# Issuing a weight piece's store, and the load that follows it, one place later in a pair

## The chip, the cores and the metric

One core of one Trainium2 chip. The metric is device time in microseconds (us) of one execution; a kernel is compared by the median of its runs. The engines are named as in the profile: PE (TensorE, its weight loads PEld), DVE (VectorE), ACT (ScalarE), POOL (GpSimd) and SP (SyncE, which here does nothing but issue transfers; its rows carry the name SPq).

## The reference, cut to what matters

A retention layer makes 2304 rows of 512 columns; a first mixture of four experts runs every row through every expert; a second mixture routes each row to one of eight experts by a greedy assignment.

```
x   = retention(q, k, v)                      # (2304, 512)
out = sum_e p[:, e] * (relu(x @ w1[e]) @ w2[e])          # first MoE, E = 4, F = 1024
logits = out @ w_gate ; assigned = greedy(logits)        # 2304 / 8 rows for each expert
out2[mask_e] = relu(out[mask_e] @ w1b[e]) @ w2b[e]       # second MoE, E = 8
```

All of it is float32.

## The kernel before

**The split.** PE works here on a reduced format, so a float32 operand is held as two tiles: a high half (ACT copies it, which rounds) and a low half (POOL or DVE subtracts). A product is then three matmuls: high by high, low by high, high by low.

**The stage of the change** is the first MoE. Its rows go through in three passes `u` of 768 rows. In a pass, 16 "pairs" `kk` follow each other; `k = 16 u + kk` counts them through (0 to 47). A pair is a quarter of an expert's hidden columns: seven block products P, Q, R of a two-by-two block scheme, in steps `a` to `g` (line L677, 6 matmuls each), and three second-layer tiles `py` (L727, 12 matmuls each) of pairs that came before, which stand after steps b, d and e. ACT copies the running sums out of the accumulators (`sum`, L684: after steps a, c and e) and makes the hidden halves (`h`, L694). Step f adds to the accumulator P that the third of these copies reads, so PE starts step f only after it. For the next pairs the kernel also prepares weights: `w1_load` (L376, L379: tiles `r`, `tw`), their split (L398, L399: `wah`, `wth`, `wbh` on ACT, `wal`, `wbl` on POOL, `wtl` on DVE), and the second-layer weights, two loads `w2_load(k, 0)` and `w2_load(k, 1)` (L659, tile `r`; `r2` in the program) and two splits `w2_split` (L664 ACT, L665 POOL or DVE).

**The job that the change touches.** While PE works on the first MoE, the weights of the second MoE are split ahead, in 128 pieces `c` of 128 x 512 (64 in pass 0, 64 in pass 1). For each piece: a load `pv` (256 KB, L433), the high half on ACT (L447) and the low half on POOL (L448), both into a tile `pair`, and a store: both halves (512 KB, L453, shown as `w_halves`) for a first-layer piece, the low half alone (256 KB, L455, `w_low`) for a second-layer piece. Eight pieces of the one kind are followed by eight of the other. The generator `halves` does, at one call: split piece `c`; store piece `c - 1`; load piece `c + 2`. It is called by `spare(True)` at five places of a pair, called A (after step a), C (ahead of step c), D (after step d), E (after step e) and E' (ahead of step f) here. `spare(False)` stands at four further places: behind `w2_load(k, 0)`, after step c, after step d, after step f; in this stage it does nothing. Tiles `pv` and `pair` have three buffers each, so the load of piece `c + 2` takes the place of piece `c - 1`.

**What sets the order.** The program is written out in the order of the loop body; each engine works through its own list in that order and waits at an instruction until what it needs is there. All transfers named here are issued by SP in one list, and all go through one queue (q1). Other members of that list are `w1_store` in pass 0 (L383, L384, `w_sums`: it follows place D and stores tiles that DVE makes), the block sums of the next pass (L869 stores, L872 to L888 loads, called behind steps c and f), and the result rows `x_rows` (L745), which wait for DVE's last addition to a row tile.

Of the kernel before, what the change touches and what calls it, by code (L numbers as in the profile page):

```python
# [327 lines left out]
def tile_kernel(ctx, tc, a, x1d, xs, ss, ts, w1s, w2s, out):  # L328
# [17 lines left out]
    if True:  # L346
# [79 lines left out]
        def piece_of(c):  # L426
            e, i = divmod(c // 2, 8)
            return e, i, slice(c % 2 * HW, c % 2 * HW + HW)

        def halves_load(c):  # L430
            e, i, o = piece_of(c)
            r = room[0].tile([128, HW], F32, name="pv")
            nc.sync.dma_start(r, (a["w1b"] if i < 4 else a["w2b"])[e, i % 4][:, o])  # L433
            HV[c] = r

        def halves(c0, c1, loaded=False):

            if not loaded:
                for c in range(c0, min(c0 + HA, c1)):
                    halves_load(c)  # L440
                yield
                yield
            for c in range(c0, c1 + 1):
                if c < c1:
                    r = HV[c]
                    pair = HV[c] = room[0].tile([128, 2, HW], F32R, name="pair")
                    nc.scalar.activation(pair[:, 0], r, AF.Copy)  # L447
                    nc.gpsimd.tensor_tensor(pair[:, 1], r, r32(pair[:, 0]), op=OP.subtract)  # L448
                if c > c0:
                    e, i, o = piece_of(c - 1)  # L450
                    pair = HV.pop(c - 1)
                    if i < 4:
                        nc.sync.dma_start(w1s[e, i][:, :, o], r32(pair))  # L453
                    else:
                        nc.sync.dma_start(w2s[e, i - 4][:, o], r32(pair[:, 1]))  # L455
                if c + HA < c1:
                    halves_load(c + HA)
                yield
# [179 lines left out]
        with ExitStack() as st:  # L638
# [17 lines left out]
            def w2_load(q, i):  # L656
                e, j = divmod(q % 16, 4)
                W2[q, i] = [hp.tile([128, 512], F32, name="r2", bufs=2)]
                nc.sync.dma_start(W2[q, i][0], a["w2a"][e, 2 * j + i])  # L659
# [190 lines left out]
            later = late()  # L850
            HC = 64
            jobs = [halves(0, HC, True), halves(HC, NH)]

            def spare(main):

                if not open_ or k < 2:
                    return
                if k > 16 * NP1 - 16:
                    next(later, None)
                elif main:  # L860
                    next(jobs[min(u, 1)], None)


            BLOCKS = {0: (0, 0), 1: (0, 1), 2: (1, 1)}
# [33 lines left out]
            for k in range(NPAIR):  # L898
                u, kk = divmod(k, 16)
# [12 lines left out]
                def block(i):  # L912
                    raw[i] = room[0].tile([128, 2, TG], F32, name=f"raw{i}")
                    if i in BLOCKS:
                        row, col = BLOCKS[i]
                        nc.sync.dma_start(raw[i], xs[u, :, 2 * col:2 * col + 2, row * TG:(row + 1) * TG])
                    else:
                        nc.sync.dma_start(raw[i], ss[u, i - 3])
# [7 lines left out]
                if k not in (1, NPAIR - 1):  # L926
                    step(k, "a")
                if turn_:
                    for _ in jobs[u]:
                        assert False  # L930
                    for _ in sums_of[u]:
                        assert False
                    st_p.close()
                    open_ = False
                    room[0] = pool(st_p, f"blocks{u}")
                    w2_load(k, 0)
                    for i in (0, 1, 4):
                        block(i)
                full = lone
                if k:  # L940
                    put(k - 1, 0, 1, "R")
                spare(True)
                step(k, "b")
                if not turn_:
                    w2_load(k, 0)
                spare(False)
                put(k, 0, 0, "Q")
                if not open_ and kk == 0:
# [4 lines left out]
                if turn_:  # L953
                    for i in (3, 5, 2, 6):
                        block(i)
                spare(True)
                step(k, "c")
                some(10 if full else 3)
# [76 lines left out]
    with ExitStack() as st:  # L1035
# [388 lines left out]
        for n, t in enumerate(range(NT - LATE, NT)):  # L1424
# [10 lines left out]
            else:  # L1435
                x = last[t - NT + K1]
# [80 lines left out]
```

## Time and profile before

| | us |
|---|---|
| median of 3 runs | 1157.22 (1154.66 to 1160.98) |
| the profiled execution | 1154.98 |
| its span | 1153.2 |
| PE busy | 1133.4 (98%) |
| ACT, POOL, DVE busy | 561.2, 632.0, 705.6 |
| q1, share of 16 engines' span | 69.3% |

The profiled execution is 1.8 us longer than its span and 2.2 us under the median. PE is busy nearly always by the page, but pipelined matmuls hide short stops in such a sum; the distance from one pair to the next shows them.

### The profile page before, as it was taken

The numbers are of one execution on the slowest core, as the hardware profiler recorded it, in microseconds if no ns is written. First come the engines' busy times: TensorE is split into PE (matmuls) and PEld (weight loads), VectorE is DVE, ScalarE is ACT, GpSimd is POOL, SyncE is SP. The second block draws the span as 40 slices with busy tenths as digits, with TensorE's granted clock in tenths as the row PEclk, the third lists the DMA queues.
The fourth block names the chain that finished last, engine by engine and source line by source line (L and its number), as shares of the span: only waits on it lengthen the run. The fifth ranks groups of instructions, "written<-read, shape, count | busy, mean of one in ns | idle before, by whom it ended". The sixth has DMA issues, their size and how long they took to land.

```text
span 1153.2 us, 22293 instructions
## 1 busy us (share of the span) xinstructions
PE 1133.4 (98%) x8007; PEld 988.5 (86%) x8007; DVE 705.6 (61%) x1632; ACT 561.2 (49%) x1262; POOL 632.0 (55%) x563
## 2 busy tenths in 40 slices
PE   9999999999999999999999999999999999999997
PEld 7878899989898998988899999998987888788886
DVE  4696777767665444544456777776347766666421
ACT  3444555555565555555554666666430333333341
POOL 4551576677774576666645999998231112222311
PEclk9999999999999999999999999999999999999999
DMA  9675699999994889898974655555214877788690
GB/s 330 219 248 176 234 338 344 322 319 321 345 309 144 279 286 335 290 310 302 316 262 158 221 181 195 192 180 158 78 55 167 311 292 284 307 332 334 252 409 27
DMA packets 131056, 292.99 MB, mean 254 GB/s; under 512 B 14849, under 2 KB 26881, under 8 KB 126849
## 3 DMA queue, kind: packets, MB, share of 16 engines
q1 hardware_dynamic: 127584, 281.88, 69.3%
q0 software_dynamic: 3216, 9.67, 2.4%
q8 instruction: 63, 1.03, 0.4%
q14 instruction: 49, 0.39, 0.1%
q10 hardware_dynamic: 144, 0.02, 0.0%
HBM read 214.41 MB, written 77.33 MB: 253 GB/s over the span
## 4 chain that ended last, share of the span: by engine, by line
PE 56%; DMA 15%; issue 5%; POOL 5%; DVE 3%; ACT 3%; SPq 3%; POOLq 0%; ACTq 0%; DVEq 0%
PE py L727 16%; PE ph L227 10%; PE P L677 9%; PE py L227 8%; PE R L677 5%; DMA r<-in_w2a 4%; DMA pv<-in_w1b 3%; DMA pv<-in_w2b 3%; DMA tw<-w_sums 3%; PE Q L677 2%; POOL pair L448 2%; PE pr L227 2%; DMA r<-in_w1a 1%; POOL w2l L665 1%; ACT pair L447 1%
## 5 line engine op out<-in xcount | busy, mean ns | idle before, releaser
L727 PE MATMUL py<-w2h,h 128*128 128x512 f32 x1056 | 349.5, 391 | 0.9 <-ACT h L694 0.8
L727 PEld LDWEIGHTS py<-w2h,h 128*128 128x128 f32 x1056 | 198.2, 188 | 40.4 <-ACT h L694 1.7
L448 POOL TENSOR_TENSOR pair<-pv,pair 128x512 fp32r<-128x512 f32 x128 | 177.3, 1391 | 97.4 <-ACT pair L447 93.4
L727 PE MATMUL py<-w2l,h 128*128 128x512 f32 x528 | 206.3, 391 | 0.0
L399 POOL TENSOR_TENSOR wal<-r,wah 128x512 fp32r<-128x512 f32 x48 | 66.8, 1392 | 87.1 <-ACT wah L398 71.8
L727 PEld LDWEIGHTS py<-w2l,h 128*128 128x128 f32 x528 | 99.2, 188 | 16.0
L684 ACT ACTIVATE sum<-P 128x384 f32<-128x384 f32 x144 | 70.0, 486 | 87.1 <-PE P L677 86.7
L665 POOL TENSOR_TENSOR w2l<-r,w2h 128x512 fp32r<-128x512 f32 x64 | 85.7, 1338 | 44.7 <-ACT w2h L664 44.7
L447 ACT ACTIVATE pair<-pv 128x512 fp32r<-128x512 f32 x128 | 80.2, 627 | 55.6 <-DMA pv<-in_w1b 27.2
L734 DVE SCALAR_TENSOR_TENSOR acc<-py,pr,acc 128x512 f32<-128x512 f32 x115 | 85.6, 745 | 29.8 <-PE py L727 29.5
L399 DVE TENSOR_TENSOR wtl<-tw,wth 128x768 fp32r<-128x768 f32 x48 | 63.5, 1322 | 64.4 <-ACT wth L398 64.2
L827 POOL TENSOR_TENSOR pp<-pw,wgb 128x512 f32<-128x512 f32 x64 | 98.5, 1560 | 1.4 <-DMA r<-in_w2a 1.4
L399 POOL TENSOR_TENSOR wbl<-r,wbh 128x512 fp32r<-128x512 f32 x48 | 81.1, 1690 | 14.6 <-ACT wbh L398 11.2
L695 DVE SCALAR_TENSOR_TENSOR h<-Q,h 128x384 fp32r<-128x384 f32 x96 | 53.4, 556 | 51.2 <-ACT h L694 51.2
L227 PE MATMUL ph<-gh,ub 128*128 128x288 f32 x512 | 83.3, 300 | 0.4 <-DVE gl L254 0.4
L664 ACT ACTIVATE w2h<-r 128x512 fp32r<-128x512 f32 x96 | 60.2, 628 | 42.2 <-DMA r<-in_w2a 42.1
L227 PEld LDWEIGHTS ph<-gh,ub 128*128 128x128 f32 x512 | 72.2, 188 | 1.2 <-DVE gl L254 0.7
L1299 POOL DMA_INDIRECT xg<-x_rows,idx x14 | 15.9, 1135 | 100.5 <-DVE idx L254 65.6
L534 ACT ACTIVATE Y<-s 64x128 f32<-64x128 f32 x128 | 33.8, 270 | 59.0 <-PE s L525 55.1
L694 ACT ACTIVATE h<-Q 128x384 fp32r<-128x384 f32 x96 | 46.7, 486 | 30.5 <-DVE Q L688 29.7
L507 POOL TENSOR_TENSOR Y<-Y,gk 64x576 f32<-64x576 f32 (+2 forms) x36 | 38.6, 1091 | 36.7 <-DMA Y<-in_kv 28.2
L523 PE MATMUL s<-X,Y 64*64 64x64 f32 x576 | 56.7, 228 | 2.0 <-DVE X L536 1.2
(272 smaller groups left out, 2667.7 us busy)
## 6 DMA issues: line engine op xcount, KB each, us to landing
w_halves<-pair SPq DMA_DIRECT2D x64, 512.0 KB, 6.0
ub<-w_halves SPq DMA_DIRECT2D x32, 1024.0 KB, 9.5
r<-in_w2a SPq DMA_DIRECT2D x96, 256.0 KB, 5.1
r<-in_w1a SPq DMA_DIRECT2D x64, 256.0 KB, 4.9
pv<-in_w1b SPq DMA_DIRECT2D x64, 256.0 KB, 5.6
pv<-in_w2b SPq DMA_DIRECT2D x64, 256.0 KB, 5.4
w_low<-pair SPq DMA_DIRECT2D x64, 256.0 KB, 4.8
raw<-in_w2b SPq DMA_DIRECT2D x32, 512.0 KB, 7.5
```

Source lines behind the costliest of these rows:

```text
L227: self.add("pe", cost, lambda: self.nc.tensor.matmul(out, w, x, start=start, stop=stop, **kw), (w, x), (out,), chain=chain, cols=self.size(x))
L399: low = lambda e, i, x: lambda: e.tensor_tensor(w(i, 1), x(), r32(w(i, 0)), op=OP.subtract)
L447: nc.scalar.activation(pair[:, 0], r, AF.Copy)
L448: nc.gpsimd.tensor_tensor(pair[:, 1], r, r32(pair[:, 0]), op=OP.subtract)
L523: nc.tensor.matmul(score()[:, h], Y[lo, h, ch(c + 1)], X[lo, h, ch(c + 1)], start=True, stop=True)
L664: nc.scalar.activation(h, r, AF.Copy)
L665: (nc.vector if i and q < 2 * NPAIR // NP1 else nc.gpsimd).tensor_tensor(lo, r, r32(h), op=OP.subtract)
L677: nc.tensor.matmul(PS[k][o][:, :TG], wx[:, c:c + 128], xx[:, kk], start=(start and n == 0), stop=(stop and n == 5), skip_group_check=True)
L684: nc.scalar.activation(sums[n], PS[k]["P"][:, :TG], AF.Copy)
L727: mm(y, x, w, start=(start and n == 0), stop=(stop and n == len(todo) - 1), **kw)
L734: nc.vector.scalar_tensor_tensor(x, y, s, x, op0=OP.mult, op1=OP.add)
L827: nc.gpsimd.tensor_tensor(pp, w[g, f], G0[e], op=OP.mult)
```

## The change

The generator yields once more, between the split of a piece and its store and load. `spare` notes that a store and a load are owed, and issues them at the next place at which it is called, whichever it is. Every piece still has the same instructions; PE, DVE, ACT and POOL have the same lists as before. Only SP's list is in another order.

```
@@ -446,6 +446,7 @@
                     pair = HV[c] = room[0].tile([128, 2, HW], F32R, name="pair")
                     nc.scalar.activation(pair[:, 0], r, AF.Copy)
                     nc.gpsimd.tensor_tensor(pair[:, 1], r, r32(pair[:, 0]), op=OP.subtract)
+                yield True
                 if c > c0:
                     e, i, o = piece_of(c - 1)
                     pair = HV.pop(c - 1)
@@ -851,14 +852,22 @@
             HC = 64
             jobs = [halves(0, HC, True), halves(HC, NH)]
 
+            owed = []
+
             def spare(main):
 
                 if not open_ or k < 2:
                     return
                 if k > 16 * NP1 - 16:
                     next(later, None)
-                elif main:
-                    next(jobs[min(u, 1)], None)
+                elif main or owed:
+
+                    job = jobs[min(u, 1)]
+                    if owed:
+                        owed.pop()
+                        next(job, None)
+                    if main and next(job, None):
+                        owed.append(True)
 
 
             BLOCKS = {0: (0, 0), 1: (0, 1), 2: (1, 1)}
@@ -926,8 +935,8 @@
                 if k not in (1, NPAIR - 1):
                     step(k, "a")
                 if turn_:
-                    for _ in jobs[u]:
-                        assert False
+                    owed.clear()
+                    assert not [x for x in jobs[u] if x]
                     for _ in sums_of[u]:
                         assert False
                     st_p.close()
```

**SP, beginning of pair 24 (pass 1).** Before; `r2` are the two second-layer weight loads, the first store and load are those issued at place A, the last two those of place C:

```order
L379 DMA tw_5668<-w1_sums 128x768
L453 DMA w1_halves<-pair_5641 256x1x512
L433 DMA pv_5687<-in_w1b 128x512
L659 DMA r2_5696<-in_w2a 128x512
L659 DMA r2_5714<-in_w2a 128x512
L453 DMA w1_halves<-pair_5683 256x1x512
L433 DMA pv_5720<-in_w1b 128x512
```

The same place of the changed program:

```order
L379 DMA tw_5668<-w1_sums 128x768
L660 DMA r2_5693<-in_w2a 128x512
L454 DMA w1_halves<-pair_5641 256x1x512
L433 DMA pv_5696<-in_w1b 128x512
L660 DMA r2_5714<-in_w2a 128x512
L454 DMA w1_halves<-pair_5683 256x1x512
L433 DMA pv_5736<-in_w1b 128x512
```

The first `r2` has moved ahead of A's store and load.

**SP, middle of pair 10 (pass 0).** Before; the stores and loads are those of places C, D and E, with a store of the block sums and `w1_store` (two rows) between them:

```order
L455 DMA w2_low<-pair_3305 128x512
L433 DMA pv_3342<-in_w2b 128x512
L869 DMA x_sums<-cx_2938 128x384
L455 DMA w2_low<-pair_3338 128x512
L433 DMA pv_3380<-in_w2b 128x512
L383 DMA w1_sums<-r1_3290 128x512
L384 DMA w1_sums<-tw_3358 128x768
L455 DMA w2_low<-pair_3376 128x512
```

The same place of the changed program:

```order
L878 DMA x_sums<-cx_2935 128x384
L456 DMA w2_low<-pair_3305 128x512
L433 DMA pv_3361<-in_w2b 128x512
L383 DMA w1_sums<-r1_3290 128x512
L384 DMA w1_sums<-tw_3355 128x768
L456 DMA w2_low<-pair_3338 128x512
L433 DMA pv_3396<-in_w2b 128x512
L456 DMA w2_low<-pair_3376 128x512
```

D's store and load have moved behind `w1_store`, C's behind the block sum.

**SP, pair 17, the first of pass 1 with pieces.** Before; `x1_rows` are result rows, the three stores and loads those of D, E and E':

```order
L453 DMA w1_halves<-pair_4522 256x1x512
L433 DMA pv_4560<-in_w1b 128x512
L745 DMA x1_rows<-acc4_1744 128x512
L453 DMA w1_halves<-pair_4556 256x1x512
L433 DMA pv_4602<-in_w1b 128x512
L745 DMA x1_rows<-acc5_1745 128x512
L453 DMA w1_halves<-pair_4598 256x1x512
```

The same place of the changed program:

```order
L746 DMA x1_rows<-acc4_1744 128x512
L454 DMA w1_halves<-pair_4522 256x1x512
L433 DMA pv_4588<-in_w1b 128x512
L746 DMA x1_rows<-acc5_1745 128x512
L454 DMA w1_halves<-pair_4556 256x1x512
L433 DMA pv_4636<-in_w1b 128x512
L454 DMA w1_halves<-pair_4598 256x1x512
```

Each result row has moved ahead of one store and load.

## Rows read from the trace of the kernel before

**Rows 1.** The page: span, and PE's busy time, share and instructions.

```profile
span 1153.2 us, 22293 instructions
PE 1133.4 (98%) x8007; PEld 988.5 (86%) x8007; DVE 705.6 (61%) x1632; ACT 561.2 (49%) x1262; POOL 632.0 (55%) x563
```

**Rows 2.** Timeline of PE, step b of pairs 2, 3, 15, 20, 30: start, length, what.

```profile
126.29 0.51 PE L677 MATMUL Q<-x1h,wah 128*128 128x384 f32 x2
...
141.77 0.51 PE L677 MATMUL Q<-x1h,wah 128*128 128x384 f32 x2
...
330.32 0.51 PE L677 MATMUL Q<-x1h,wah 128*128 128x384 f32 x2
...
416.77 0.51 PE L677 MATMUL Q<-x1h,wah 128*128 128x384 f32 x2
...
576.91 0.51 PE L677 MATMUL Q<-x1h,wah 128*128 128x384 f32 x2
```

**Rows 3.** Waits of PE's weight loads, 126 to 331 us: total, times, longest.

```profile
PEld P L677 <- ACT sum L684: 2.1, 3, 1.3
PEld R L677 <- DVE Q L688: 1.1, 2, 0.9
```

**Rows 4.** The same, 416 to 577 us.

```profile
PEld P L677 <- ACT sum L684: 5.8, 7, 1.3
```

**Rows 5.** Timeline of all engines in pair 24: in brackets idle time and its ender.

```profile
482.68 0.54 SPq L453 DMA_DIRECT2D w_halves<-pair  x1
...
483.93 2.04 SPq L659 DMA_DIRECT2D r<-in_w2a  x2
...
487.97 0.85 ACT L398 ACTIVATE wth<-tw 128x768 fp32r<-128x768 f32 x1 [1.01 <-DMA tw<-w_sums]
...
488.73 0.61 ACT L398 ACTIVATE wbh<-r 128x512 fp32r<-128x512 f32 x1
...
489.42 1.55 POOL L399 TENSOR_TENSOR wbl<-r,wbh 128x512 fp32r<-128x512 f32 x1 [1.08 <-ACT wbh L398]
...
490.52 0.63 ACT L664 ACTIVATE w2h<-r 128x512 fp32r<-128x512 f32 x1 [1.18 <-DMA r<-in_w2a]
...
491.06 0.61 ACT L447 ACTIVATE pair<-pv 128x512 fp32r<-128x512 f32 x1
...
491.23 1.27 POOL L665 TENSOR_TENSOR w2l<-r,w2h 128x512 fp32r<-128x512 f32 x1 [0.27 <-ACT w2h L664]
...
491.58 0.47 ACT L684 ACTIVATE sum<-P 128x384 f32<-128x384 f32 x1
...
492.10 0.62 PE L677 MATMUL P<-x2h,wth 128*128 128x384 f32 x2 [0.41 <-ACT sum L684]
...
493.79 0.54 SPq L453 DMA_DIRECT2D w_halves<-pair  x1
```

**Rows 6.** Timeline in pairs 10 and 11: SP, ACT, POOL, PE.

```profile
261.00 0.33 SPq L433 DMA_DIRECT2D pv<-in_w2b  x1
...
263.00 0.32 SPq L384 DMA_DIRECT2D w_sums<-tw  x1
...
266.32 0.63 ACT L447 ACTIVATE pair<-pv 128x512 fp32r<-128x512 f32 x1
...
269.13 2.59 POOL L448 TENSOR_TENSOR pair<-pv,pair 128x512 fp32r<-128x512 f32 x2
...
270.81 0.51 PE L677 MATMUL P<-x4h,wth 128*128 128x384 f32 x2
```

**Rows 7.** Line L433 (the loads `pv`), all 128: time from issue to landing.

```profile
DMA to landing us min/median/max: 2.9/5.4/7.4
```

**Rows 8.** Timeline of SP in pair 17.

```profile
377.35 0.54 SPq L453 DMA_DIRECT2D w_halves<-pair  x1
...
381.45 0.33 SPq L745 DMA_DIRECT2D x_rows<-acc  x1
```

**Rows 9.** Stretches: length, busy time by engine, PE's clock share, DMA share, GB/s.

```profile
141.77:157.25 15.48, 15.48 (x80) 14.04 (x79) 11.29 (x18) 9.06 (x17) 11.06 (x9) 1.00 1.00 365
```

More of the change, by code (lines that the diff above doesn't have):

```diff
@@ L448, in halves @@
                     nc.gpsimd.tensor_tensor(pair[:, 1], r, r32(pair[:, 0]), op=OP.subtract)
+                yield True
                 if c > c0:
@@ L852, in tile_kernel @@
             jobs = [halves(0, HC, True), halves(HC, NH)]
+            owed = []
             def spare(main):
@@ L859, in spare @@
                     next(later, None)
-                elif main:
-                    next(jobs[min(u, 1)], None)
+                elif main or owed:
+                    job = jobs[min(u, 1)]
+                    if owed:
+                        owed.pop()
+                        next(job, None)
+                    if main and next(job, None):
+                        owed.append(True)
             BLOCKS = {0: (0, 0), 1: (0, 1), 2: (1, 1)}
@@ L928, in tile_kernel @@
                 if turn_:
-                    for _ in jobs[u]:
-                        assert False
+                    owed.clear()
+                    assert not [x for x in jobs[u] if x]
                     for _ in sums_of[u]:
```

## The prediction

> **What bounds the kernel now.** The page first: PE is busy 98% of 1153.2 us [rows 1], so only work taken from PE, or stops of PE, can move the time; the change takes no work away. The stops have to be looked for in the stage where SP's list changes, and busy time hides them there. The second view is therefore the timeline of PE at one fixed instruction of each pair, the first matmul of step b. An undisturbed pair takes 141.77 - 126.29 = 15.48 us [rows 2]. In pass 0, pairs 2 to 14 take 330.32 - 126.29 = 204.03 us, 13 x 15.48 would be 201.24: 2.8 us are lost. In pass 1, pairs 20 to 29 take 160.14 us instead of 154.8: 5.3 us are lost. Together 8.1 us, 0.7% of the kernel, and that is all that a better order of transfers can return. The third view, PE's waits, says for what it stops: for ACT's copy `sum` of accumulator P, seven times in pass 1 [rows 4], three times in pass 0, where step g also waits twice for DVE [rows 3].
>
> The fourth view shows why the copy is late: all engines in pair 24 [rows 5]. ACT stands idle 1.18 us until a second-layer weight of the first MoE (`r`, the first of SP's two loads at 483.93) has landed. Only then come `w2h` at 490.52, place D's `pair` at 491.06 and `sum` at 491.58, and PE's step f goes on at 492.10. That load was issued behind place A's store (482.68) and A's load `pv`. The stop thus ends with a transfer, and the change moves exactly this one two places forward in SP's list.
>
> **What the move ahead of A's store is worth.** `tw`, which stands just before A's store, lands when `wth` starts (487.97), the weight when `w2h` starts (490.52) [rows 5]: 2.55 us for store, load and weight, 512 + 256 + 256 KB. If they land in the order of issue, the weight, with a quarter of these bytes, lands after 0.64 us, near 488.6. ACT reaches it when `wbh` is done, near 489.3, so the wait of 1.18 us is gone. But the next thing on ACT is place D's `pair`, and its `pv` is the load of place A. It now lands last of the three, where the weight landed before: 490.5. So the stall is passed on: not the weight is late next, but D's piece. What is won is the slot that `w2h` took behind the landing, 491.06 - 490.52 = 0.54 us: `pair` at 490.5, `sum` at 491.0, PE at 491.6 instead of 492.1.
>
> There is a second, smaller gain. SP's next burst of transfers starts with place E's store (493.79), which waits for POOL's low half of D's piece. POOL goes `wbl` (ends 490.97), `w2l` after 0.27 us of waiting for ACT's `w2h`, `pair`, then the store [rows 5]. With `w2h` early POOL runs on from `wbl`: the burst starts 0.27 us sooner, and in pass 1, where a late burst makes the next `tw` and weight late, this adds up.
>
> *Pass 1.* The lag that makes the seven stops is carried from pair to pair, so the 0.54 us counts once and the 0.27 us up to seven times: 0.54 + 7 x 0.27 = 2.4 us. Against it stands the start of pass 1. E's store stood ahead of a result row and left at 377.35; now it stands behind one that SP issues at 381.45, when DVE's addition is done [rows 8]. Its store and load, 768 KB, have to go in the burst that follows. At the 365 GB/s of the fullest pair [rows 9] these are 2.15 us at most; nothing, if the queue was empty anyway. I take 1.0, about the middle, since the trace has no row for it. Pass 1 gives 1.4 us; its bounds are nothing (2.4 less 2.15, and less than that if the 0.27 is not passed on) and all 5.3.
>
> *Pass 0.* Here the stops stand alone. The three waits for `sum` sum to 2.1 us with 1.3 as the longest [rows 3], so the other two together are 0.8. Cut by 0.54 each, they return 0.54 from the longest and at most 0.8 from the others: 1.3; the waits of step g for DVE, 1.1 us in two, come from the same late `sum` and shrink with it. PE loses 2.8 in all; I take half, 1.4. Bounds: 0.5 (one slot) and 2.8.
>
> **What the moves behind other transfers cost.** In pass 0, D's store and load now stand behind `w1_store`, whose second row SP issues at 263.00 when DVE has made the tile. D's load left at 261.00 before [rows 6]; with `w1_store` and the store of about 0.33 us each ahead of it, it leaves near 263.8, 2.8 us later. Its user is the copy of place E' (266.32, no wait: the load took under 5.3 us). Behind that copy on ACT stand the hidden half `h` of step f and the first `sum` of the next pair, and PE's step c of that pair needs this `sum` at 270.81. Copy, `h` and `sum` take about 0.63 + 2 x 0.49 = 1.6 us, so the load may land until 269.2, 5.4 us after its issue. On POOL the piece has its turn only at 269.13, 2.8 us after the copy began, behind `wbl`; that cover hides all but a few tenths. I cost this move at nothing: the same bytes stand ahead of the load as before, minus 2.8 us in which the queue went on, so it should land sooner after its issue than the 5.3 us it had. If it doesn't, PE pays in each of twelve pairs (the last loads nothing); this is the rival below.
>
> The Trainium skill, "DMA: Bandwidth & Descriptors", section "Rules for kernel authors", advises to issue a transfer early and to wait for it late. The change does the opposite for every `pv`, and the rule counts against it. By that rule the time is the slower rival's below. No row so far shows ACT stopping PE at place E', so the rule and these rows differ.
>
> C's pair of transfers moves behind a stored block sum, whose tile DVE has made one place before, and E' behind up to three loads of 192 KB in a few pairs. At 365 GB/s the three take 1.6 us [rows 9]. What they make late is the next pair's place C, whose copy is followed by `sum` for step e; step e is two steps and a `py` later. Costed at nothing. SP's own time is no matter: the same rows are issued.
>
> **The sum.** 1.4 + 1.4 = 2.8 us. Against the profiled execution's own time that is 1154.98 - 2.8 = 1152.2, against the median of runs, 2.2 us higher, 1154.4. The three runs lie 6.3 us apart, so neither is better; I forecast the middle, **1153.3 us**.
>
> **Rivals.**
> - *All stops go.* If the weight's landing is the only link and D's `pv` is not missed (landing nearly together with the weight), and the bursts move forward by more than 0.27, then all 8.1 us return: 1146.9 from the profiled time, 1149.1 from the median. For it: ACT's wait before `w2h` is in each stopped pair the last one. Against it: D's copy follows the weight at once, and its load now lands last.
> - *The order doesn't matter because the transfers are the bound.* Pair 3 moves 365 GB/s with the DMA engines busy throughout [rows 9]. If the stopped pairs lack bandwidth and not order, the gain is the slot alone, 0.5 us and less: 1154.5 from the profiled time, about 1156.5 from the median. Against it: pair 3 takes 15.48 us all the same [rows 2]. The Trainium skill, same page, section "Specifications", gives about 358 GB/s as a core's share of memory bandwidth; the row lies at that.
> - *Slower: D's load lands too late for the next pair.* Its place is E' of pass 0, its point of decision a landing 5.4 us after issue. The median of all `pv` is just that, the longest 7.4 [rows 7]. At 6.4, midway, PE stops 1.0 us in each of twelve pairs: 12 us more, less the 2.8: about 1164. At 7.4 it would be 24 us. For it: the rows of all places leave no margin. Against it: the load at this very place took under 5.3 us with a fuller queue.
>
> **How the numbers follow.** My forecast 0.56, with its own range from 1150.5 (5 us gained on the profiled time) to 1157; all stops gone 0.17; no effect 0.13; slower 0.14. About 0.5% (5.8 us) is what a measurement of this kernel can tell from no change. Against the median of 1157.2 this is reached below 1151.4: all of the first rival and a small edge of the forecast, 0.21. Slower by more than 0.5%, over 1163: most of the last rival, 0.12. The rest, 0.67, is within. The range leaves out the lower end of the first rival and the greater part of the last: 1147.5 to 1160.
>
> **What would show it.** Right: in pass 1 ACT's wait for `r` before `w2h` is nearly gone and a wait for `pv` stands before D's `pair` instead, at the same distance behind `tw`; PE's waits for `sum` there fall from 5.8 us to about 4; pairs 20 to 29 take 158 to 159 us. In pass 0 the E' copies wait 1 to 3 us for `pv` and PE has no new stop in step c. Wrong: stops of PE in step c or in the first `py` of a pair in pass 0; bursts that begin later behind the result rows of pair 17 and never catch up; or D's `pair` not waiting at all, and all stops gone.

## The result, and the profile after

The changed kernel takes 1173.19 us (median; 1170.93 to 1177.5) beside 1159.1 us of the kernel before, four executions of each: a ratio of 1.0128, 95% interval 1.009 to 1.0167, so about 14.8 us slower by the ratio; the medians lie 14.1 us apart. The forecast was 1153.3 us, at most 1160. The profiled execution took 1170.93 us. From L449 on, line numbers are one to nine higher than before.

The page, where [rows 1] stood:

```profile
span 1169.2 us, 22285 instructions
PE 1136.7 (97%) x8007; PEld 987.8 (84%) x8007; DVE 719.1 (62%) x1632; ACT 559.6 (48%) x1262; POOL 631.7 (54%) x563
```

Busy time says nearly nothing: PE's is 3 us longer, the span 16. The timeline of PE at step b of pairs 2, 15, 20 and 30, as in [rows 2], says where it went:

```profile
126.25 0.51 PE L678 MATMUL Q<-x1h,wah 128*128 128x384 f32 x2
...
346.17 0.51 PE L678 MATMUL Q<-x1h,wah 128*128 128x384 f32 x2
...
432.64 0.51 PE L678 MATMUL Q<-x1h,wah 128*128 128x384 f32 x2
...
592.70 0.51 PE L678 MATMUL Q<-x1h,wah 128*128 128x384 f32 x2
```

Pairs 2 to 14 take 219.92 us instead of 204.03: 15.9 us, as much as the spans differ. Pairs 20 to 29 take 160.06 instead of 160.14. So in these two profiles the whole loss lies in pass 0.

What PE's weight loads wait for in pass 0 (126 to 347 us: total, times, longest), beside [rows 3]:

```profile
PEld py L728 <- ACT h L695: 10.1, 6, 3.6
PEld R L678 <- DVE Q L689: 6.4, 5, 1.7
PEld P L678 <- ACT sum L685: 2.7, 3, 1.8
```

The first line is new: `py`, a second-layer tile, waits for ACT's hidden half `h`. The second, step g, stood before with 1.1 us; it is read further down. The prediction looked for a new stop in step c as well, and none is there beyond the third line, which stood before with 2.1 us. The three lines come to 19.2 us, 16.0 more than their 3.2 before: that is the loss. A stop of the first kind, pairs 9 and 10, on SP, ACT, DVE and PE; it answers to [rows 6]:

```profile
254.44 0.33 SPq L383 DMA_DIRECT2D w_sums<-r  x1
256.80 0.33 SPq L384 DMA_DIRECT2D w_sums<-tw  x1
257.21 0.54 SPq L454 DMA_DIRECT2D w_halves<-pair  x1
257.81 0.60 SPq L433 DMA_DIRECT2D pv<-in_w1b  x1
...
263.20 0.63 ACT L447 ACTIVATE pair<-pv 128x512 fp32r<-128x512 f32 x1 [3.61 <-DMA pv<-in_w1b]
263.73 0.47 ACT L695 ACTIVATE h<-P 128x384 fp32r<-128x384 f32 x1
...
264.24 0.56 DVE L696 SCALAR_TENSOR_TENSOR h<-P,h 128x384 fp32r<-128x384 f32 x1 [3.76 <-ACT h L695]
264.71 0.88 DVE L888 TENSOR_TENSOR cx<-xt,cx 128x384 f32<-128x384 f32 x1
265.51 0.55 DVE L689 TENSOR_TENSOR R<-R,sum 128x384 f32<-128x384 f32 x1
...
266.10 0.49 ACT L695 ACTIVATE h<-R 128x384 fp32r<-128x384 f32 x1 [1.51 <-DVE R L689]
...
266.64 0.50 PE L728 MATMUL py<-w2h,h 128*128 128x512 f32 x1 [3.23 <-ACT h L695]
```

Read it upwards. PE stands 3.23 us until `h` of R is there; ACT waited for DVE's R; DVE stood 3.76 us for ACT's `h` of P; ACT stood 3.61 us at place E' for the piece that place D had loaded; that load left only at 257.81, because it stands behind `w1_store`, and SP waited at both of its rows for DVE. This is SP's total of such waits in pass 0 after (first three rows) and before (last three):

```profile
SPq L384 <- DVE tw L397: 31.9, 13, 3.1
SPq L383 <- DVE r L397: 26.7, 12, 3.0
SPq L456 <- POOL pair L448: 11.3, 13, 1.9
```

```profile
SPq L455 <- POOL pair L448: 26.3, 24, 2.8
SPq L384 <- DVE tw L397: 9.5, 11, 2.0
SPq L383 <- DVE tw L397: 8.5, 8, 1.6
```

Before, SP spent its idle time waiting for POOL, in front of stores, and 18.0 us in front of `w1_store`. Now it stands 58.6 us there, with D's load behind. And over the first pairs it grows. `w1_store`'s second row in pairs 3 to 5, the step b of pairs 4 and 5, and what DVE does ahead of pair 5's `tw`:

```profile
151.15 0.33 SPq L384 DMA_DIRECT2D w_sums<-tw  x1
...
157.21 0.33 PE L678 MATMUL Q<-x1h,wah 128*128 128x384 f32 x1
...
169.04 0.32 SPq L384 DMA_DIRECT2D w_sums<-tw  x1
...
173.05 0.51 PE L678 MATMUL Q<-x1h,wah 128*128 128x384 f32 x2
...
177.93 0.56 DVE L696 SCALAR_TENSOR_TENSOR h<-P,h 128x384 fp32r<-128x384 f32 x1 [5.21 <-ACT h L695]
...
183.05 1.01 DVE L397 TENSOR_TENSOR tw<-r,r 128x256 f32<-128x256 f32 x1
...
188.39 0.32 SPq L384 DMA_DIRECT2D w_sums<-tw  x1
```

Counted from its pair's step b this row leaves at 9.4 us in pair 3 (step b at 141.73), 11.8 in pair 4, 15.3 in pair 5. Late `h` on ACT and DVE make DVE's next `tw` late, that makes `w1_store` late, and that D's next load: a loop. It doesn't run on: from pair 6 to pair 14 the row leaves between 11.4 and 14.3 us and one time at 15.1; before, all pairs lay between 8.5 and 13.3.

DVE's steps for `tw` have also become longer. The group L397, 26 instructions in pass 0 (busy, mean ns of one): before, then after.

```profile
L397 DVE TENSOR_TENSOR tw<-r,tw 128x256 f32<-128x256 f32 x26 | 18.3, 703 | 0.5
```

```profile
L397 DVE TENSOR_TENSOR tw<-r,tw 128x256 f32<-128x256 f32 x26 | 32.9, 1265 | 0.4
```

Two of them make the last parts of a `tw`, so each `tw` comes 1.1 us later by these two. Over pairs 2 to 13 the first step of a `tw` begins 7.0 us after step b before and 7.5 us after, the last one 9.5 and 11.5 us (means of starts in the timeline): of the 2.1 us by which `w1_store` leaves later, about 0.5 are DVE's later start, where the loop would show, and 1.5 the longer steps. Pair 8 shows why they are longer: DVE and POOL before, and then in the changed kernel pair 7, with ACT and PE at its end:

```profile
226.34 1.29 POOL L399 TENSOR_TENSOR wal<-r,wah 128x512 fp32r<-128x512 f32 x1 [0.85 <-ACT wah L398]
...
228.65 0.88 DVE L397 TENSOR_TENSOR tw<-r,tw 128x256 f32<-128x256 f32 x2
...
230.37 1.29 POOL L665 TENSOR_TENSOR w2l<-r,w2h 128x512 fp32r<-128x512 f32 x1 [2.74 <-ACT w2h L664]
```

```profile
218.53 1.47 POOL L399 TENSOR_TENSOR wal<-r,wah 128x512 fp32r<-128x512 f32 x1
219.97 1.48 POOL L666 TENSOR_TENSOR w2l<-r,w2h 128x512 fp32r<-128x512 f32 x1
...
220.21 2.95 DVE L397 TENSOR_TENSOR tw<-r,tw 128x256 f32<-128x256 f32 x2
...
220.58 0.47 ACT L685 ACTIVATE sum<-P 128x384 f32<-128x384 f32 x1
221.41 1.47 POOL L448 TENSOR_TENSOR pair<-pv,pair 128x512 fp32r<-128x512 f32 x1
...
223.75 0.55 DVE L689 TENSOR_TENSOR Q<-R,sum 128x384 f32<-128x384 f32 x1
...
224.35 0.62 PE L678 MATMUL R<-x6h,wbh 128*128 128x384 f32 x2 [1.34 <-DVE Q L689]
```

Before, POOL stood idle 2.74 us between `wal` and `w2l`, because the weight had not landed (ACT's `w2h` waited 3.39 us for it), and DVE made its two steps in that gap, 0.88 us for both. With the weight loaded ahead of place A's store POOL runs without a gap, and the same two steps take 2.95 us. The Trainium skill, "SBUF — State Buffer", section "SBUF: two separate sides", says that a DVE operation with two SBUF inputs and a GpSimd operation that reads SBUF exclude each other for a whole instruction. The trace agrees: two such subtractions take 0.88 us in POOL's gap and 2.95 us beside POOL, and each of the 26 takes either 0.41 to 0.43 us or 1.39 to 1.53 us, in both kernels.

The longer steps also reach PE directly. In pair 7 ACT's `sum` is there at 221.05, but DVE's addition to Q, which reads it, comes behind the two steps and starts at 223.75; PE's step g waits for it. In all five stops of step g DVE came to Q without a pause, 2 to 4 us after the `sum` was there.

### The profile page after: what moved, and what is told of

It reads as the page before. It is cut to its first block, busy times and chain, and to the rows that moved or that the text cites. A ratio compares the mean times of both kernels' runs of the same rounds, so it can differ in the third digit from the quotient of the medians.

```text
span 1169.2 us, 22285 instructions
## 1 busy us (share of the span) xinstructions
PE 1136.7 (97%) x8007; PEld 987.8 (84%) x8007; DVE 719.1 (62%) x1632; ACT 559.6 (48%) x1262; POOL 631.7 (54%) x563
## 4 chain that ended last, share of the span: by engine, by line
PE 56%; DMA 12%; issue 5%; DVE 5%; POOL 3%; ACT 2%; SPq 1%; POOLq 0%; ACTq 0%; DVEq 0%
PE py L728 17%; PE ph L227 10%; PE P L678 9%; PE py L227 8%; PE R L678 4%; DMA pv<-in_w1b 4%; DMA r<-in_w1a 3%; DMA pv<-in_w2b 3%; PE Q L678 2%; DVE tw L397 2%; PE pr L227 2%; POOL pair L448 1%; DMA r<-w_sums 1%; PE ph L231 1%; ACT pair L447 1%
## 5 line engine op out<-in xcount | busy, mean ns | idle before, releaser
L448 POOL TENSOR_TENSOR pair<-pv,pair 128x512 fp32r<-128x512 f32 x128 | 173.5, 1358 | 134.5 <-ACT pair L447 128.9
L399 DVE TENSOR_TENSOR wtl<-tw,wth 128x768 fp32r<-128x768 f32 x48 | 56.5, 1178 | 57.7 <-ACT wth L398 57.4
L399 POOL TENSOR_TENSOR wbl<-r,wbh 128x512 fp32r<-128x512 f32 x48 | 81.7, 1702 | 15.9 <-ACT wbh L398 12.5
L1308 POOL DMA_INDIRECT xg<-x_rows,idx x14 | 15.9, 1135 | 100.5 <-DVE idx L254 65.6
L696 DVE SCALAR_TENSOR_TENSOR h<-P,h 128x384 fp32r<-128x384 f32 x48 | 26.6, 554 | 52.6 <-ACT h L695 52.4
```

Source lines behind the costliest of these rows:

```text
L399: low = lambda e, i, x: lambda: e.tensor_tensor(w(i, 1), x(), r32(w(i, 0)), op=OP.subtract)
L696: nc.vector.scalar_tensor_tensor(hl, c, 0.0, r32(hh), op0=OP.max, op1=OP.subtract)
```

## The experiments

Theory one: place D's move behind `w1_store` makes the loss, in a loop. Theory two: place A's move (the earlier weight) makes it, through POOL beside DVE's `tw` steps. A rival to theory two: A's own load is late, so that place D's copy comes late on ACT. In the kernels below a place is moved only where a condition holds; elsewhere it stores and loads at once, as before. `main` is the place's name (E' is "X") and `u` the pass:

```diff
                     if main and next(job, None):
-                        owed.append(True)
+                        if CONDITION:
+                            owed.append(True)
+                        else:
+                            next(job, None)
```

The executions differ by up to 10 us ahead of this stage (see the last section), so profiles are compared by the length of pairs 2 to 14, "pass 0", and times by ratios. A ratio of 1.001 is 1.2 us. Each kernel has one profile, and pass 0 differs between executions too: the run with pass 1 alone moved has the pass 0 of before and took 202.93 us there instead of 204.03.

**Without D, D alone, A alone, pass 1 alone.** The conditions are `main != "D" or u`, `main == "D" and u == 0`, `main == "A"` and `u`.

> The changed kernel, but in pass 0 place D issues its store and load at once again, so they stand ahead of w1_store; all other places stay moved. Theory one (D's pair of transfers behind w1_store is the whole loss: the load comes too late, which makes the next w1_store late, and so on round): the 15.9 us that pass 0 lost against before are gone; pairs 2 to 14 take 203 to 205 us instead of 219.9, and the time is that of before within 3 us. Theory two (the weight that now comes earlier puts POOL's work beside DVE's steps for tw and so makes w1_store late by itself): the steps of L397 stay near 1.0 to 1.5 us, w1_store stays late, and pairs 2 to 14 stay over 212 us.

> The kernel before, with one move alone: in pass 0 place D's store and load go behind w1_store. Theory one (that move is the whole loss): pairs 2 to 14 take 217 to 222 us instead of 204.0, the time is 13 to 18 us over before, ACT's copy at place E' waits 2 to 5 us for its piece. Theory two (the earlier weight makes w1_store late): the weight isn't moved here, so pairs 2 to 14 stay within 203 to 207 us and the time within 3 us of before. If both are needed, it lies between: 207 to 215 us.

> The kernel before, with one move alone: place A's store and load go behind the first second-layer weight, in both passes. The forecast's own reckoning of this move: 0.5 us for the slot and 0.27 us for each of seven bursts, so pairs 20 to 29 take 157.5 to 159 us instead of 160.1, and the time is 1 to 4 us less than before. Theory two (an earlier weight puts POOL beside DVE and makes w1_store late): pass 0 slower, pairs 2 to 14 over 207 us. Theory three (the place of the weight's landing on ACT's list is only handed to D's piece): nothing in either pass, 203 to 205 and 160 us.

> The changed kernel with the moves in pass 1 alone; pass 0 is as before. Theory one and theory two, both of which put the whole loss in pass 0: within 2 us of before, pairs 2 to 14 take 204 us and pairs 20 to 29 160 us. If the loss of pass 0 hid a gain of pass 1 (pass 1 began later and with fuller buffers in the changed kernel), pairs 20 to 29 take 156 to 159 us and the time is 1 to 4 us less than before.

Measured: without D in pass 0, 1.0009 (0.9984 to 1.0034), pass 0 203.49 us. D alone, 1.0076 (1.0047 to 1.0104), 207.73 us. A alone, 0.9988 (0.9965 to 1.001), 203.82 us. Pass 1 alone, 0.9984 (0.9955 to 1.0014), pairs 20 to 29 160.73 us. So D's move is needed for the loss, and the first run fits theory one as it was put. D alone makes only 8.8 of the 14.8 us, though (in its profile pass 0 lost 3.7 of 15.9), and its `w1_store` leaves on average no later than before (10.3 us after step b, 10.6 before), so theory one's loop is not enough: something among the other moves adds to it. A's move costs nothing by itself, though the steps of L397 are long there as well:

```profile
L397 DVE TENSOR_TENSOR tw<-r,tw 128x256 f32<-128x256 f32 x26 | 28.8, 1107 | 0.4
```

The later `tw` has no one behind it as long as D's load stands ahead of `w1_store`. The moves of pass 1 are worth nothing that these times can tell: their interval reaches from 5.2 us less to 1.6 more, that of A alone from 4.1 less to 1.2 more, so A's gain of 1 to 4 us is neither shown nor excluded. Pairs 20 to 29 of A alone took 156.47 us in its profile, even less than the 157.5 to 159 expected, and 157.31 in a second kernel with A alone (with early `tw`, below). The kernels whose pass 1 is as before took 158.05 to 161.65 us there, those with all moves in pass 1 156.52 to 161.38, so single profiles don't settle it either.

**Which part of D, and A with and without D.** In the first two kernels D's load, or D's store, is issued at once and the other half is moved, with all other places moved:

```diff
+                if mode:
+                    store() if mode == "store" else load()
                 yield True
...
+                if mode != "store":
+                    store()
+                if mode != "load":
+                    load()
                 yield
```

The other two have the conditions `u or main != "A"` and `u == 0 and main in ("A", "D")`.

> The changed kernel, but in pass 0 place D's load is issued at once, ahead of w1_store, and only its store goes behind. Theory one a (the load is what comes too late, and the copy at place E' passes that on): the loss is gone, pairs 2 to 14 take 203 to 205 us, the time is that of before within 4 us. Theory one b (what hurts is that a store and the stores behind it are held up at SP, so later transfers are late, whichever transfer of D stands there): the loss stays, pairs 2 to 14 over 212 us and 10 us or more over before.

> The mirror of the run before: the changed kernel, but in pass 0 place D's store is issued at once and only its load goes behind w1_store. Theory one a (the late load): the loss stays, pairs 2 to 14 take 212 to 222 us and the time is 10 to 18 us over before. Theory one b (the held-up store): the loss is gone, 203 to 205 us, the time within 4 us of before.

> The changed kernel, but place A isn't moved in pass 0; C, D, E and E' are. D's move alone cost 8.8 us by the runs and the whole change 14.8, so something among the others adds 6. If it is A's (the weight that comes earlier puts POOL beside DVE, theory two as a helper): this kernel costs what D alone does, 7 to 11 us over before, and L397's steps in pass 0 are shorter than in the changed kernel. If it is C, E or E' (loads that are later at their own place too): 13 to 17 us over before.

> The mirror of the run before: the kernel before, with A and D moved in pass 0 and nothing else. If A's move adds the 6 us to D's: 13 to 17 us over before, pairs 2 to 14 over 215 us. If C, E or E' add them: 7 to 11 us, 207 to 211 us.

Measured: load in place 1.0011 (0.9983 to 1.004), 206.60 us; store in place 1.0063 (1.003 to 1.0096), 211.09 us; without A 1.005 (1.0025 to 1.0075), 206.37 us; A and D 1.0111 (1.0047 to 1.0174), 217.08 us. With D's load ahead of `w1_store` the loss is gone by the ratio (2.6 us in pass 0 of the profile), so the late load carries it. With the load alone behind, half of it is there, less than expected; the store, when it stands ahead of the load, may delay that further (the load leaves at 13.6 us after step b instead of 12.7). Without A the loss is 5.8 us, and its interval lies apart from that of the whole change; with A and D alone it is 12.9, with a wide interval. A's move adds only where D's is made.

**Does A add by POOL's work?** The first kernel makes all moves but puts DVE's last two `tw` steps behind step c:

```diff
-                some(10 if full else 3)
+                some(10 if full else 5 if k + 1 < 16 else 3)
...
-                some(3)
+                some(1 if 0 < k < 15 else 3)
```

The next two do POOL's `wal` twice in pass 0, with D moved and with no place moved. The last moves A alone, with the `tw` steps as in the first.

> The changed kernel with all its moves, but in pass 0 DVE's last two steps for tw (L397) stand with the first two, behind step c and ahead of the block-sum addition and of POOL's wal, instead of behind step d. Theory (w1_store is late because POOL's w2l, which the earlier weight has moved forward, lies beside those two steps, and D's load is late because it stands behind w1_store): the two steps take about 0.42 us each instead of 1.41, w1_store's second row leaves 2 to 4 us sooner after step b than the 12.6 us of the changed kernel, and pairs 2 to 14 take 203 to 208 us instead of 219.9; the time is at most 5 us over before. If the place of w1_store's issue plays no part, because D's and E's loads only lack transfer time: 215 us and more, 12 us or more over before.

> The kernel before with D alone moved in pass 0 (that alone cost 8.8 us), and POOL's wal done twice over in pass 0, the second time with the same result: POOL works beside DVE's tw steps as it does behind the earlier weight, but no weight comes earlier. Theory (A's move adds to the loss only by that overlap): L397's last steps go from 0.42 to about 1.4 us, and the time is 12 to 17 us over before, as with A and D together (13). If the overlap plays no part and A's move works through its later load: 7 to 10 us over before.

> The control to the run before: the kernel before with no transfer moved, POOL's wal done twice in pass 0. Theory: the longer L397 steps make w1_store about 1 us later, but D's load stands ahead of it, so the time is within 3 us of before, like A's move alone. If the doubled instruction costs by itself (POOL late for its stores): 5 us or more over before, and the run before has to be read against this one.

> A version that could beat both: the kernel before with A alone moved in both passes, and DVE's last two tw steps placed with the first two in pass 0. Theory: with the overlap out of the way the earlier weight is worth what the forecast reckoned for pass 0 and pass 1, 2 to 5 us less than before; pairs 2 to 14 take 201.3 to 202.5 us. If PE's stops of pass 0 come from the pieces of place C that wait for their loads, nothing: 203 to 204 us, the time within 2 us of before.

Measured: 1.0098 (1.0062 to 1.0134), 216.12 us; D and POOL 1.016 (1.0113 to 1.0207), 216.71 us; POOL alone 1.0059 (1.0034 to 1.0085), 210.06 us; A with early `tw` 1.0006 (0.9982 to 1.003). By their times none of them decides it. The first edit failed to do what it was for: 20 of the 26 steps are still long, 18 of them beside POOL's `w2l` or low half of a piece, their mean is 1218 ns, and `w1_store` came only 1.6 us sooner. Doubling `wal` did lengthen the steps (1262 ns, from 653 with D alone), but costs 6.8 us by itself, so the 18.5 us of the second prove no more than a sum of 8.8 and 6.8. PE's waits say more: `py` waits 8.1 us for `h` there, 4.0 with D alone and not at all with POOL alone (table below). So more work on POOL beside the `tw` steps adds to D's loss, though no weight comes earlier and D's copy waits for no load; part of it may come by way of POOL's own delay. And the version that was to beat both kernels does not.

**A's store or A's load.** As for D above, now for A in pass 0, with all other places moved; and last the kernel before with every load ahead of its store.

> The changed kernel, but in pass 0 place A's load goes ahead of the second-layer weight, and only A's store behind it. Without A's move the changed kernel cost 5.8 us more than before, with it 14.8, so A's move adds about 9 where D's is made too. Theory two (the weight that comes earlier puts POOL beside DVE's last two tw steps): the weight is still ahead of the 512 KB of the store, so those steps stay at 1.4 us and the time is 11 to 17 us over before. Rival (A's load, which feeds D's copy, is late; ACT waits 0.7 to 1.3 us for it in most pairs of the changed kernel): the load is in place, so D's copy waits under 0.3 us and the time is 4 to 8 us over before.

> The mirror of the run before: A's store stays ahead of the second-layer weight, only A's load goes behind it. Theory two: the weight lands nearly as late as before, DVE's last two tw steps take 0.42 us in half of the cases or more, and the time is 4 to 8 us over before. Rival (A's late load): D's copy waits as in the changed kernel, and the time is 11 to 17 us over before.

> The kernel before, no place moved, but at every place, in both passes, the load is issued ahead of the store instead of behind it. If the landing of the loads is what ACT and so PE wait for at the stops that are left before (8.1 us), each load now has 256 or 512 KB less ahead of it, 0.7 to 1.4 us at 365 GB/s: 2 to 6 us less than before. If those stops follow from the weight r and from POOL, which are not moved: within 2 us of before.

Measured: 1.0103 (1.0063 to 1.0144), 214.57 us; 1.0104 (1.0062 to 1.0146), 213.52 us; 1.0014 (0.999 to 1.0039), 201.93 us. The first two don't separate store from load, since even behind one of the two transfers the weight comes early enough to close POOL's gap: the steps' means are 1055 and 973 ns. The expectation of 0.42 us in the second was wrong. In both, D's copy waits for its piece 0.4 us on average, less than half of the changed kernel's 1.0, and the loss is still 12 us: that speaks against the rival, A's late load. Loads ahead of stores gain nothing, though pass 0 of this profile lost only 0.7 us: the stops of the kernel before are worth less than the noise.

**The overlap removed, the late loads kept.** All transfers as in the change; in pass 0 the weight's split stands behind place D's copy, which waits for A's late load, so POOL has its gap again:

```diff
-                w2_split(k, 0)
+                if u:
+                    w2_split(k, 0)
                 spare("D")
+                if not u:
+                    w2_split(k, 0)
```

> The changed kernel with all its moves, transfers in the same order, but in pass 0 the first weight's split (w2h on ACT, w2l on POOL) stands behind place D's copy instead of ahead of it. D's copy still waits for A's load, which is as late as in the changed kernel, and holds w2h up; so POOL should idle behind wal, as it did before, while DVE makes its last two tw steps. Theory two (A's move adds to the loss by POOL's work beside those steps): they take 0.42 us in most pairs again, and the time is 4 to 8 us over before, as without A's move. Rival (A's move adds by its late load): the load is untouched, so the time stays 11 to 17 us over before, whatever the steps take.

Measured: 1.0016 (0.9991 to 1.0042). By the ratio nearly the whole loss is gone, more than theory two asked, with D's copy waiting 1.1 to 2.7 us in most pairs. DVE and POOL in pair 9, and L397's group:

```profile
250.67 1.28 POOL L399 TENSOR_TENSOR wal<-r,wah 128x512 fp32r<-128x512 f32 x1 [0.55 <-ACT wah L398]
...
253.16 0.88 DVE L397 TENSOR_TENSOR tw<-r,tw 128x256 f32<-128x256 f32 x2
...
254.05 1.29 POOL L448 TENSOR_TENSOR pair<-pv,pair 128x512 fp32r<-128x512 f32 x1 [2.09 <-ACT pair L447]
```

```profile
L397 DVE TENSOR_TENSOR tw<-r,tw 128x256 f32<-128x256 f32 x26 | 20.2, 779 | 0.4
```

The gap is back and so are the 0.88 us. The rival, A's late load, falls: ACT waited for that load no less than in the changed kernel. The traces had spoken against it already: D's copy begins 9.7 us after step b in the changed kernel and 9.2 with A and D, but 9.9 before and 9.8 with D alone (means over pairs 2 to 13), so late as A's load is, it doesn't make that copy later. The profile is of the longest execution of this kernel (1166.61 us, median 1162.04), and its pass 0 of 209.96 us lost 5.9 us, as theory two asked; how pass 0 went in the others is not known. `py` waits 4.8 us in it, as with D alone (4.0) and all but A (4.5). The edit also puts D's copy and its low half ahead of `w2h` and `w2l`; the kernel before with that order alone was not run.

All kernels in one table. When D's load left and when the copy at E' began are given as means over pairs 2 to 13, in us after that pair's step b, worked out from the starts in the timeline; then come the mean of L397's two steps in ns, PE's waits in pass 0 of `py` for ACT's `h` and of step g for DVE's Q (totals in us, from the view of PE's weight loads), the length of pass 0 and the ratio.

| kernel | D's load | E' copy | L397 | `py` | step g | pass 0 | ratio |
|---|---|---|---|---|---|---|---|
| loads first | 6.9 | 13.9 | 539 | 0 | 0 | 201.93 | 1.0014 |
| before | 8.1 | 14.3 | 703 | 0 | 1.1 | 204.03 | 1 |
| A alone | 7.5 | 14.3 | 1107 | 0 | 2.5 | 203.82 | 0.9988 |
| pass 1 alone | 8.0 | 14.2 | 501 | 0.5 | 0 | 202.93 | 0.9984 |
| all but D | 7.7 | 14.5 | 1147 | 0.2 | 2.0 | 203.49 | 1.0009 |
| A, early `tw` | 7.3 | 14.2 | 1213 | 1.2 | 2.1 | 204.51 | 1.0006 |
| POOL alone | 7.5 | 14.5 | 1098 | 0 | 4.5 | 210.06 | 1.0059 |
| D's load in place | 7.3 | 15.8 | 1106 | 1.5 | 3.5 | 206.60 | 1.0011 |
| all but A | 11.8 | 16.3 | 699 | 4.5 | 0 | 206.37 | 1.005 |
| D alone | 11.3 | 16.3 | 653 | 4.0 | 1.6 | 207.73 | 1.0076 |
| split behind D | 11.6 | 16.6 | 779 | 4.8 | 2.8 | 209.96 | 1.0016 |
| D's store in place | 12.7 | 17.0 | 1190 | 4.3 | 5.7 | 211.09 | 1.0063 |
| early `tw` | 12.0 | 16.8 | 1218 | 8.6 | 3.8 | 216.12 | 1.0098 |
| A's load late | 12.5 | 17.3 | 973 | 7.3 | 3.7 | 213.52 | 1.0104 |
| A and D | 12.7 | 17.5 | 1174 | 8.9 | 4.8 | 217.08 | 1.0111 |
| A's store late | 12.6 | 17.5 | 1055 | 7.8 | 2.2 | 214.57 | 1.0103 |
| D and POOL | 13.3 | 17.9 | 1262 | 8.1 | 5.3 | 216.71 | 1.016 |
| changed | 13.6 | 18.3 | 1265 | 10.1 | 6.4 | 219.92 | 1.0128 |

On the whole, the later the copy at E' begins, the longer the pass, from about 15 us on. D's place alone makes it late by 2 us, and `py` then waits 4 to 5 us in all; where the L397 steps are long as well, it is late by 0.5 to 2 more. Where D's load stands ahead of `w1_store` it is not late, but for the kernel with D's load in place (15.8), which was not followed up. Except with D's store in place, long steps and D's late load together bring the waits of `py` to 7.3 us and more. The waits of step g go with the long steps: at most 2.8 us in the six kernels with a mean under 800 ns, 2.0 to 6.4 in the others; POOL alone, which loses 6 us, has 4.5 there and none at `py`.

## Why the prediction was wrong

- **What bounds the kernel: half right.** PE's stops and ACT's late copies were the right place to look. But the reading stopped at the engines that wait; SP, whose list the change reorders, was read for what it issues and not for where it stands. It stood 18.0 us ahead of `w1_store` in pass 0 already, as the view of its own waits shows.
- **The failed step: "I cost this move at nothing", D's load behind `w1_store`.** Two numbers in it were off. The load was to leave 2.8 us later; it left 5.5 us later (8.1 to 13.6 us after step b), because the time of `w1_store` was taken over from the kernel before and moved itself by 2.1 us (10.6 to 12.6), most of it by the longer `tw` steps. The deadline was a landing at 269.2, 2.2 us after step b of pair 11 (267.03), since step c of that pair was taken for the user, though the first `py` of a pair is among the prediction's signs of being wrong. In every second pair that `py` comes first, by way of the copy at E', `h` of P, DVE's R, `h` of R and `py`. In pair 9 PE was ready at 266.64 - 3.23 = 263.41, and from copy to `py` are 3.44 us, so the copy had to begin at 259.97, 0.2 us before step b of pair 10 (260.16): 2.4 us earlier than reckoned. What the step said of the landing held, though its count of the bytes was wrong (`w1_store`'s 640 KB now stand ahead of the load): the load "should land sooner after its issue", and the copies, all of which waited for it, began 4.7 us after it on average, where it had landed after 5.6 us before (eleven of the twelve loads have a landing in that trace). It was late because it left late. The rival that ends slower had the right place and the right transfer, with a chance of 0.14. That its price (12 us, a time of 1164) comes near is in part luck: it was for a load that lands 6.4 us after its issue, and the part that A's move adds is not in it.
- **"No row so far shows ACT stopping PE at place E'".** That was the trace of an order in which it did not. The rule of the Trainium skill to issue early and wait late ("DMA: Bandwidth & Descriptors", "Rules for kernel authors"), which the prediction set aside for these rows, agrees with the run that put D's load alone back: 1.0011 instead of 1.0128.
- **The move ahead of A's store: the link right, the worth open.** In pair 24 `w2h` no longer waits, and D's `pair` waits 0.76 us and starts 2.65 us behind `wth` (507.10 and 508.48 below); the forecast was 2.53, and it was 3.09 [rows 5].

```profile
505.83 0.85 ACT L398 ACTIVATE wth<-tw 128x768 fp32r<-128x768 f32 x1 [1.37 <-DMA tw<-w_sums]
...
507.10 0.62 ACT L665 ACTIVATE w2h<-r 128x512 fp32r<-128x512 f32 x1
508.48 0.63 ACT L447 ACTIVATE pair<-pv 128x512 fp32r<-128x512 f32 x1 [0.76 <-DMA pv<-in_w1b]
...
509.54 0.62 PE L678 MATMUL P<-x2h,wth 128*128 128x384 f32 x2 [1.60 <-ACT sum L685]
```

- But `tw` itself came 10.4 us after step b (495.42) instead of 8.8, so PE stops 1.60 us there instead of 0.41. In this pair the slot of 0.54 us was won and the burst ahead of it lost; by the two profiles pass 1 gained 0.1 us, not 1.4, and the run with pass 1 alone shows nothing either. The two profiles with A alone show 3.7 and 2.8 us, but pass 1 differs that much between profiles, so the worth is not known. The same holds for the 1.4 us of pass 0: 203.82 us with A alone, 204.03 and 202.93 in the two profiles with nothing moved there. PE's waits for `sum` fell as foretold, to the row below from 5.8 us [rows 4], and 2.7 us of waits for `h` took their place. Why the burst was late, the result rows of pair 17 or something else, was not tested.

```profile
PEld P L678 <- ACT sum L685: 3.6, 3, 2.0
PEld py L728 <- ACT h L695: 2.1, 2, 1.7
PEld py L728 <- DVE h L696: 0.6, 2, 0.3
```

- **"With `w2h` early POOL runs on from `wbl`" was counted as a gain alone.** In pass 0 it also runs on from `wal`, beside DVE, and there it cost: by the runs this is what turns the 5.8 to 8.8 us of D into 14.8, through a later `w1_store` (and so D's load) and through step g, whose waits went from 1.1 to 6.4 us. The prediction had no term for it.
- **C behind the sums, E' behind the loads: nothing,** as far as the run without D shows.

What stays open: the kernel with the split behind D shows hardly any loss by its ratio (interval up to 1.0042), though its E' copies begin as late as with D alone (from 1.0047). The interval of all but A (1.0025 to 1.0075) overlaps it, and its own profile lost 5.9 us in pass 0, so it is not shown that anything in it gives back what D's place costs; the order of D's copy and `w2h` on ACT was not tried alone.

## What to carry to other kernels

When an issue moves past another in an in-order queue, ask first what that other one waits for, and whether it will wait longer once the moved one is late: here SP stood at a store of DVE's tile, that tile came later once POOL's gap had closed, and the load behind it fed the chain that PE's next second-layer tile waits for. Follow the consumer through every engine it passes, to the first one that PE needs, not to the one found first. And an instruction made ready earlier is not free if it runs on POOL while DVE reads two SBUF operands: a gap on one can be the other's speed.

## What the runs showed of the hardware

Two subtractions of 128x256 on DVE took 0.88 us while POOL was idle and 2.95 us beside POOL's subtractions of 128x512, which themselves took 1.47 instead of 1.29 us. Of the 468 such subtractions (L397's last two of each `tw`) in pass 0 of the eighteen profiles every one took either 0.41 to 0.43 us or 1.37 to 1.56 us, nothing between.

Executions of one program differ by some 10 us before this stage begins: step b of pair 2 is at 126.25 us in the changed kernel and at 136.77 in the one that moves D alone. Windows of that one (length, busy time of PE, PEld, DVE, ACT, POOL, PE's clock share, DMA share, GB/s):

```profile
90.00:100.00 10.00, 8.83 (x179) 7.18 (x176) 7.09 (x18) 4.78 (x16) 2.13 (x2) 0.96 0.65 196
100.00:110.00 10.00, 9.62 (x101) 7.12 (x97) 5.45 (x13) 2.19 (x6) 2.02 (x8) 0.50 0.58 164
```

The granted clock fell to 0.50, the level of 1.2 GHz, after a stretch in which PE was busy 8.83 of 10 us. In the kernel before it stayed at 1.00, with PE busy 9.38 us in the same window, and in the one with all but A too, with 8.73 us, so this share alone doesn't tell the cases apart. A difference of two spans says nothing here before this stage has been set apart.
